# A planned attention and two gated MLPs on one core: the planner's prices and passes, and the making of the masks

## The chip, the cores and the metric

One core of a Trainium2 chip. Its engines run instruction streams of their own: TensorE (PE in the profile, its weight loads PEld), VectorE (DVE), ScalarE (ACT), GpSimd (POOL) and SyncE (SP), which issues most transfers. The metric is device microseconds of one execution of the whole program.

## The reference

Windowed attention over 2 batches, 8 heads and 768 rows: each row sees the 96 rows up to itself and the first 8 keys, with a bias that falls with the distance at a slope of its own for each head. Then two gated MLPs.

```python
def _attn_ref(q, k, v, n_global, n_local):
    scores = scale * np.matmul(q, k.transpose(0, 1, 3, 2))
    rel = pos[:, None] - pos[None, :]
    is_global = pos[None, :] < int(n_global)
    is_local = (rel >= 0) & (rel < int(n_local))
    keep = is_global | is_local
    dist = np.where(is_global & ~is_local, float(n_local), np.abs(rel).astype(np.float32))
    slopes = 2.0 ** (-8.0 * (np.arange(H, dtype=np.float32) + 1) / H)
    scores = np.where(keep, scores - slopes[:, None, None] * dist, -1000000000.0)
    scores = scores - np.max(scores, axis=-1, keepdims=True)
    a = np.exp(scores)
    a = a / (np.sum(a, axis=-1, keepdims=True) + 1e-09)
    return np.matmul(a, v)

x = attention, heads side by side                            # 2 x 768 x 512
gate = sigmoid(causal convolution of x, 5 taps, conv_w)
x = (gate * (x @ w_val)) @ w_out                             # 512 -> 512
h = relu(x @ w_in)                                           # 512 -> 1024
gate = sigmoid(centred convolution of h, 3 taps, conv_w)
out = (h * gate) @ w_out2                                    # 1024 -> 512
```

## The kernel before

The attention is done in twelve tiles of 128 rows (six a batch). A tile has its scores against its own and the previous 128 keys (`scores`, s on the page; the first 8 keys are copied into the keys that a tile reads, `first_keys`, L474). VectorE adds the head's mask and takes the row's extreme in one instruction (`least`, L441), ScalarE makes the exponentials with their sum (`grow`), GpSimd adds the small constant (`guard`, L457), VectorE inverts the sum (`invert`, L460) and scales each head (`on_dve`, L467). TensorE transposes the heads (`turn`, L491, tile t), ScalarE copies them (L495), and TensorE multiplies by the values (`output`, L509, tile x). Scores, transposes and output use TensorE's array in different shapes: 64x128, 128x128 and 128x64 rows by columns (64\*128, 128\*128 and 128\*64 in a row of the page). The first tile of a batch has only its own 128 keys (masks b, or `B0`), the others 256 (masks `B`). The former are made from a distance `d0`, the latter from `d`, by one instruction of GpSimd a head (`mask_head`).

The MLPs go over four chunks (two a batch, 400 and 368 columns with their overlap). `hidden_inputs` splits x into two parts of lower precision and starts the gate; `values` multiplies by w_val; `hidden` multiplies by W, the product of the first w_out and w_in that `product` makes on the chip; `project` multiplies by the last w_out. A large product is three matmuls (`mm3`, L219 to L221), of a high part and a remainder (`split_ops`: ScalarE L210, VectorE L212; tiles gx, gg and g). A gate (`conv_gate`) has its first tap on ScalarE (L616) or on GpSimd (L617), its further taps on VectorE (L621) and a tanh on ScalarE; VectorE multiplies by it. Weights come as 64-bit floats and are rebuilt as 32-bit ones by four instructions (`to_f32`: ScalarE, GpSimd L240, VectorE L245 and L248).

What runs when is not the program's order. Every piece is a `Work` with an engine and a price (or several engines with a price each), and a `Plan` lays them out before anything is issued. A pass from the end backward (`lay(..., True)`) gives each its rank; a pass forward takes, on the engine that is free first, the work of the least rank among those that can start, at its price, with a delay of `LAG` between engines and 0.1 for a change of TensorE's array (`SWITCH`). `issue` then emits all work in the order of the planned starts, and each engine keeps to that order. The prices are simple formulas:

```python
def act_us(n, psum=False, sums=False):
    return 0.115 + 0.000714 * n + 0.09 * sums

def pool_us(n):
    return 0.12 + 0.0018 * n
```

A load has a price of 0.5 on SyncE and a delay of 2 to 4 until it has landed. The buffers are rings (`c.ring`): four banks of PSUM for s, one each for t and x, two for f; two buffers `o` for what leaves at the end. The last block of 128 output rows goes in two halves of 256 columns, the second copied by VectorE (L771) into an `o` that must have been written out before.

## Time and profile before

| | |
|---|---|
| median of 3 runs | 297.78 us (297.34 to 299.58) |
| the profiled execution | 296.97 us |
| its span in the profile | 295.2 us |
| TensorE busy | 271.7 us, 92% of the span |
| VectorE busy | 238.3 us, 81% |
| ScalarE busy | 198.8 us, 67% |
| GpSimd busy | 57.4 us, 19% |

The span is what the trace shows from its first to its last record; the execution's time has 1.8 us around it. A busy share is one over the whole span, and where in it an engine has no gap is read from stretches of 10 us.

### The profile page before, as it was taken

To read this page: it belongs to the slowest core of one execution; us is meant where nothing else is said; L and a number is where in the kernel's file an instruction comes from. 1 tells how busy PE (TensorE), PEld (TensorE's weight loads), DVE (VectorE), ACT (ScalarE), POOL (GpSimd) and SP (SyncE) were. 2 spreads that over 40 slices of the span, in tenths; PEclk is the share of its full clock that TensorE was granted. 3 is DMA by queue.
4 is the path that set the end of the run, shared out by engine and by line. 5 is a ranking of instruction groups with operands and counts; after the bars stand their busy time and mean duration, and the time that the engine had idled before them with its cause. 6 is when DMAs were issued, how large, how long until landed. Compare 5 with 4: busy or idle time off the path is not lost.

```text
span 295.2 us, 5444 instructions
## 1 busy us (share of the span) xinstructions
PE 271.7 (92%) x1832; PEld 227.5 (77%) x1832; DVE 238.3 (81%) x638; ACT 198.8 (67%) x498; POOL 57.4 (19%) x153
## 2 busy tenths in 40 slices
PE   2398897999998999999999999999999999999990
PEld 2366775664554699999898899989999988999890
DVE  4789998899999999999799999999996643367500
ACT  2589999998386879798689663895466523466410
POOL 2831112234211210032212440011220200000000
PEclk9999999999999999999999999999999999999998
DMA  4953478564514521002412000000000000000111
GB/s 139 361 221 112 149 255 273 180 194 163 165 52 142 154 107 38 19 2 95 151 49 71 2 1 36 3 0 36 36 2 37 36 2 36 36 2 3 71 73 44
DMA packets 10277, 26.18 MB, mean 89 GB/s; under 512 B 1408, under 2 KB 2688, under 8 KB 10240
## 3 DMA queue, kind: packets, MB, share of 16 engines
q1 hardware_dynamic: 9440, 25.22, 25.1%
q10 hardware_dynamic: 800, 0.52, 0.6%
q8 instruction: 16, 0.26, 0.4%
q14 instruction: 21, 0.17, 0.2%
HBM read 22.59 MB, written 3.15 MB: 87 GB/s over the span
## 4 chain that ended last, share of the span: by engine, by line
PE 75%; DMA 8%; ACT 5%; issue 4%; DVE 3%; SPq 2%; POOL 1%; POOLq 0%; DVEq 0%; ACTq 0%
PE f L295 8%; PE f L219 8%; PE s L220 7%; PE s L221 7%; PE s L219 7%; PE f L221 7%; PE f L220 7%; PE x L509 4%; PE t L491 3%; PE s L430 3%; ACT p L446 3%; DMA v<-in_v_dram 3%; PE x L221 2%; PE t L221 2%; PE x L219 2%
## 5 line engine op out<-in xcount | busy, mean ns | idle before, releaser
L446 ACT ACTIVATE p<-p,st 128x256 f32<-128x256 f32 (+1 forms) x96 | 46.0, 483 | 7.8 <-DVE st L441 7.7
L621 DVE SCALAR_TENSOR_TENSOR z<-h,cw,z 128x384 f32<-128x384 f32 x64 | 39.9, 633 | 8.5 <-ACT z L616 7.1
L220 PE MATMUL s<-w,g 128*128 128x512 f32 (+1 forms) x104 | 39.5, 379 | 0.0
L221 PE MATMUL s<-w,g 128*128 128x512 f32 (+1 forms) x104 | 39.2, 377 | 0.0
L219 PE MATMUL s<-w,g 128*128 128x512 f32 (+1 forms) x104 | 39.1, 376 | 0.0
L623 ACT ACTIVATE z<-z 128x384 f32<-128x384 f32 (+2 forms) x48 | 25.0, 523 | 18.8 <-DVE z L621 18.8
L491 PE MATMUL t<-ident,p 128*128 128x128 f32 x176 | 29.0, 284 | 8.9 <-DVE p L467 4.8
L621 DVE SCALAR_TENSOR_TENSOR z<-x,cw,z 128x400 f32<-128x400 f32 (+1 forms) x64 | 36.9, 616 | 0.0
L491 PEld LDWEIGHTS t<-ident,p 128*128 128x128 f32 x176 | 20.2, 142 | 20.5 <-ACT pts L495 8.5
L441 DVE CUSTOM_DVE_ANT_0 p<-s,B 128x256 f32<-128x256 f32 x80 | 30.9, 414 | 3.7 <-POOL kq L474 1.4
L467 DVE TENSOR_SCALAR p<-p,st 128x256 f32<-128x256 f32 (+1 forms) x96 | 31.8, 369 | 0.4
L295 PE MATMUL f<-w,w 128*128 128x512 f32 x64 | 30.8, 604 | 0.0
L495 ACT ACTIVATE pts<-t 128x512 f32<-128x512 f32 (+1 forms) x48 | 26.5, 551 | 5.6 <-PE t L491 3.6
L219 PE MATMUL f<-gg,Wh 128*128 128x400 f32 (+1 forms) x80 | 27.7, 347 | 0.0
L221 PE MATMUL f<-gg,Wl 128*128 128x400 f32 (+1 forms) x80 | 27.1, 338 | 0.0
L220 PE MATMUL f<-gg,Wh 128*128 128x400 f32 (+1 forms) x80 | 27.0, 338 | 0.0
L212 DVE TENSOR_TENSOR g<-z,g 128x384 fp32r<-128x384 f32 x32 | 17.4, 551 | 9.9 <-ACT g L210 9.9
L430 PE MATMUL s<-kq 64*128 64x128 f32 x320 | 24.1, 289 | 0.5 <-POOL kq L474 0.5
L430 PEld LDWEIGHTS s<-kq 64*128 64x128 f32 x320 | 20.3, 193 | 4.7 <-issue 2.7
L509 PE MATMUL x<-pts,v 128*64 128x128 f32 x320 | 22.1, 278 | 2.0 <-ACT x L526 1.2
L240 POOL TENSOR_SCALAR raw<-raw 128x512 f32<-128x512 f32 x24 | 18.1, 757 | 28.9 <-ACT m L238 19.3
L734 DVE SCALAR_TENSOR_TENSOR z<-z,h 128x384 f32<-128x384 f32 x32 | 18.0, 565 | 5.7 <-ACT z L623 5.6
(117 smaller groups left out, 595.2 us busy)
## 6 DMA issues: line engine op xcount, KB each, us to landing
raw<-in_moe_w_out_dram SPq DMA_DIRECT2D x12, 512.0 KB, 3.5
kq<-in_kq_dram SPq DMA_DIRECT2D x11, 512.0 KB, 4.7
raw<-in_moe_w_in_dram SPq DMA_DIRECT2D x8, 512.0 KB, 4.0
v<-in_v_dram SPq DMA_DIRECT2D x11, 256.0 KB, 4.5
...
raw<-in_moe_w_val_dram SPq DMA_DIRECT2D x4, 512.0 KB, 3.4
...
```

Source lines behind the costliest of these rows:

```text
L219: nc.tensor.matmul(out, lh, rh, start=first, stop=False)
L220: nc.tensor.matmul(out, lh, rl, start=False, stop=False)
L221: nc.tensor.matmul(out, ll, rh, start=False, stop=last)
L295: nc.tensor.matmul(ps.t, big["wot"].t.bitcast(F32)[:, e, cs], big[wi].t.bitcast(F32)[:, e, :], start=e == 0, stop=e == 3)
L430: nc.tensor.matmul(out, keys(t0, pr, 1)[hs], keys(j, pr, 0)[hs], start=True, stop=True)
L441: nc.vector.tensor_tensor_reduce(w.t[:, :nk], sc, bias, -QKSCALE, 3.0e38, ALU.add, ALU.min, st.t[:, 0, h : h + 1])
L446: nc.scalar.activation(w.t[:, :nk], w.t[:, :nk], AF.Exp, bias=st.t[:, 0, h : h + 1], scale=-1.0, accum_out=st.t[:, 1, h : h + 1],)
L467: nc.vector.tensor_scalar(w.t[:, :nk], w.t[:, :nk], st.t[:, 2, h : h + 1], None, ALU.mult)
L491: nc.tensor.transpose(o[:, z, n, :], p[2 * pr + z].t[:, n * P : (n + 1) * P], ident)
L495: nc.scalar.activation(w.t[:, :, :nw, :], o[:, :, :nw, :], AF.Copy)
L509: nc.tensor.matmul(o[z * D : (z + 1) * D, pr, :], vals(j, 2 * pr + z), pts[pr].t[:, z, n, :], start=n == 0, stop=n == len(js) - 1,)
L621: nc.vector.scalar_tensor_tensor(z(), src(k), w()[:, k : k + 1], z(), ALU.mult, ALU.add)
```

## The change

The planner: new prices for each kind of instruction (ScalarE dearer for a sum, for a scale and for a source in SBUF; a tap on GpSimd 0.17 + 0.0013 a column instead of 0.12 + 0.0018), loads priced by their kilobytes with one delay of 2.4 until they have landed, and times at which the engines can begin (`START`). `lay` adds 3.0 to the rank of TensorE's work that would change the array's shape (`STICK`). `issue` repeats the two passes six times, each backward pass with the ends of the forward pass before as its ranks, and keeps the order, and the choice of engines, of the pass whose planned end is earliest.

The masks: GpSimd writes the positions as floats at once, with those behind the row replaced by a large number (`positions`); VectorE makes the first distance in three instructions instead of eight and the second (`distance`) in three instead of five. Each head's mask may be made by GpSimd, ScalarE or VectorE, as the planner chooses (`head_ways`, `any`); the first two heads are no longer made ahead of the branch that picks this arm of the kernel.

```diff
@@ -84,7 +85,10 @@
 
 
     LAG = {"PE": 0.2, "ACT": 0.15, "DVE": 0.15, "POOL": 0.15, "SP": 0.0}
+    START = {"DVE": 0.4, "ACT": 1.2, "SP": 0.3}
     SWITCH = 0.1
+    STICK = 3.0
+    PASSES = 6
 
     def __init__(self):
         self.work, self.wrote, self.read, self.rings = [], {}, {}, []
...
+    def any(self, ways, bufs=(), reads=(), writes=()):
+        e = next(iter(ways))
+        us, fn = ways.pop(e)
+        return self.add(e, us, fn, bufs, reads, writes, **ways)
+
...
@@ -131,6 +140,7 @@
         left = {w: len(pred(w)) for w in self.work}
         ready = {e: [] for e in self.LAG}
         free = dict.fromkeys(self.LAG, 0.0)
+        free.update({} if back else self.START)
         mode, est, at = None, dict.fromkeys(self.work, 0.0), {}
 
         def enter(w):
...
@@ -150,7 +160,7 @@
                 ws = [w for w in ws if len(w.ways) == 1 or here(w, e)]
                 if ws:
                     t = max(free[e], min(est[w] for w in ws)) + 0.02
-                    w = min((w for w in ws if est[w] <= t), key=rank)
+                    w = min((w for w in ws if est[w] <= t), key=lambda w: rank(w) + (self.STICK if not back and e == "PE" and w.mode != mode else 0.0))
                     t = max(free[e], est[w])
                     if best is None or t < best[0]:
                         best = t, w, e
...
@@ -177,23 +187,33 @@
         self.link()
         order = list(self.work)
         if laid:
-            back = self.lay(lambda w: w.succ, lambda w: w.pred, lambda w: 0.0, True)
-            for w in self.work:
-                w.rank = -back[w] - w.cost + w.bias
-            at = self.lay(lambda w: w.pred, lambda w: w.succ, lambda w: w.rank, False)
-            order.sort(key=lambda w: at[w])
+            after, best = dict.fromkeys(order, 0.0), None
+            for _ in range(self.PASSES):
+                back = self.lay(lambda w: w.succ, lambda w: w.pred, lambda w: -after[w], True)
+                for w in order:
+                    w.rank = -back[w] - w.cost + w.bias
+                at = self.lay(lambda w: w.pred, lambda w: w.succ, lambda w: w.rank, False)
+                after = {w: at[w] + w.cost for w in order}
+                end = max(after.values())
+                if best is None or end < best[0]:
+                    best = end, at, {w: w.eng for w in order}
+            end, self.at, engs = best
+            for w in order:
+                w.eng = engs[w]
+                w.cost = w.ways[w.eng][0]
+            order.sort(key=lambda w: self.at[w])
         for w in order:
             for b in w.opens:
                 b.t = b.ring.make()
             w.ways[w.eng][1]()
 
 
-def act_us(n, psum=False, sums=False):
-    return 0.115 + 0.000714 * n + 0.09 * sums
-
-
-def dve_us(n, extra=0.07):
-    return extra + 0.00104 * n
+def act_us(n, sbuf=True, scaled=False, sums=False):
+    return 0.05 + 0.000834 * n + 0.042 * sbuf + 0.092 * scaled + 0.093 * sums
+
+
+def dve_us(n, scaled=False):
+    return 0.069 + 0.001042 * n + 0.061 * scaled
 
 
 def pe_us(n):
...
@@ -201,15 +221,19 @@
 
 
 def pool_us(n):
-    return 0.12 + 0.0018 * n
-
-
-def split_ops(c, hi, lo, src, n, bufs, reads, writes):
+    return 0.17 + 0.0013 * n
+
+
+def dma_us(kb):
+    return max(0.4, kb / 385.0)
+
+
+def split_ops(c, hi, lo, src, n, bufs, reads, writes, sbuf=True):
 
...
-    pl.add("ACT", act_us(n), lambda: nc.scalar.activation(hi(), src(), AF.Copy), bufs, reads, [writes + ("hi",)])
+    pl.add("ACT", act_us(n, sbuf), lambda: nc.scalar.activation(hi(), src(), AF.Copy), bufs, reads, [writes + ("hi",)])
...
@@ -326,13 +350,18 @@
 def scratch(c):
 
     x = [c.x[:, d, XP:] for d in range(NC1)]
-    c.rel, c.ge, c.loc, c.d = (x[d][:, 0:WIN] for d in range(4))
-    c.key, c.k0, c.d0, ic = (x[d][:, 4 * P : 5 * P] for d in range(4))
-    return c.d.bitcast(I32), ic.bitcast(I32)
-
-
-def mask_head(c, out, d, h):
-    c.nc.gpsimd.tensor_scalar(out, d, -slope(h) / QKSCALE, 1.0, ALU.mult, ALU.mult)
+    c.rel, c.w, c.d = (x[d][:, 0:WIN] for d in range(3))
+    c.key, c.far, c.d0 = (x[d][:, 4 * P : 5 * P] for d in range(3))
+
+
+def positions(c):
+
+    nc = c.nc
+    nc.gpsimd.iota(c.rel, pattern=[[-1, WIN]], base=P, channel_multiplier=1, allow_small_or_imprecise_dtypes=True)
+    nc.gpsimd.iota(c.key, pattern=[[1, P]], base=0, channel_multiplier=0, allow_small_or_imprecise_dtypes=True)
+    nc.gpsimd.affine_select(
+        out=c.rel, in_=c.rel, compare_op=ALU.is_ge, fill=BIG, base=P, pattern=[[-1, WIN]], channel_multiplier=1
+    )
 
 
 def first_mask(c):
@@ -341,38 +370,40 @@
     lf = c.small.tile([P, 2], F32, name="lf")
     nc.vector.tensor_copy(lf, c.li[:, :, 0])
     c.ng, c.nl = ng, nl = lf[:, 0:1], lf[:, 1:2]
-    rel, loc, key, k0, d0 = c.rel, c.loc, c.key, c.k0, c.d0
-    nc.vector.scalar_tensor_tensor(loc, rel, nl, c.ge, ALU.is_lt, ALU.mult)
-    nc.vector.scalar_tensor_tensor(d0, rel[:, P:], nl, loc[:, P:], ALU.subtract, ALU.mult)
-    nc.vector.scalar_tensor_tensor(k0, key, ng, loc[:, P:], ALU.is_lt, ALU.max)
-    nc.vector.tensor_scalar(k0, k0, -BIG, BIG, ALU.mult, ALU.add)
-    nc.vector.scalar_tensor_tensor(d0, d0, nl, k0, ALU.add, ALU.add)
-    c.b0 = c.const.tile([P, 2, P], F32, name="b0")
-    c.B0 = [c.b0[:, h, :] for h in range(2)]
-    for h in range(2):
-        mask_head(c, c.B0[h], d0, h)
+    rel, w = c.rel[:, P:], c.w[:, P:]
+    nc.vector.tensor_scalar(c.far, c.key, ng, BIG, ALU.is_ge, ALU.mult)
+    nc.vector.scalar_tensor_tensor(w, rel, nl, c.far, ALU.is_ge, ALU.mult)
+    nc.vector.scalar_tensor_tensor(c.d0, rel, nl, w, ALU.min, ALU.add)
+
+
+def head_ways(c, n, out, d, h):
+
+    nc, k = c.nc, -slope(h) / QKSCALE
+    return {
+        "POOL": (0.02 + pool_us(n), lambda: nc.gpsimd.tensor_scalar(out(), d, k, 1.0, ALU.mult, ALU.mult)),
+        "ACT": (act_us(n), lambda: nc.scalar.activation(out(), d, AF.Copy, scale=k)),
+        "DVE": (0.07 + 0.00052 * n, lambda: nc.vector.tensor_scalar(out(), d, k, None, ALU.mult)),
+    }
 
 
 def masks(c, ap):
 
     nc, pl = c.nc, c.plan
-    ng, nl, rel, loc, d, key = c.ng, c.nl, c.rel, c.loc, c.d, c.key
+    ng, nl, rel, w, d = c.ng, c.nl, c.rel, c.w, c.d
     c.B = ap.tile([P, NH, WIN], F32, name="B")
-    b0 = ap.tile([P, NH - 2, P], F32, name="b02")
-    c.B0 += [b0[:, h, :] for h in range(NH - 2)]
-    for h in range(2, NH):
-        pl.add("POOL", 0.33, lambda h=h: mask_head(c, c.B0[h], c.d0, h), [], ["d0"], [("B0", h)])
+    b0 = ap.tile([P, NH, P], F32, name="b0")
+    c.B0 = [b0[:, h, :] for h in range(NH)]
+    for h in range(NH):
+        pl.any(head_ways(c, P, lambda h=h: c.B0[h], c.d0, h), [], ["d0"], [("B0", h)])
 
     def distance():
-        nc.vector.tensor_scalar(key[:, 0:GW], key[:, 0:GW], ng, None, ALU.is_lt)
-        nc.vector.tensor_scalar(d, loc, -BIG, BIG, ALU.mult, ALU.add)
-        nc.vector.tensor_scalar(d[:, 0:GW], key[:, 0:GW], -BIG, BIG, ALU.mult, ALU.add)
-        nc.vector.tensor_tensor(d[:, GW:], d[:, GW:], rel[:, GW:], ALU.add)
-        nc.vector.tensor_scalar(d[:, 0:GW], d[:, 0:GW], nl, None, ALU.add)
-
-    pl.add("DVE", 1.1, distance, [], [], ["d"])
+        nc.vector.tensor_scalar(w[:, GW:], rel[:, GW:], nl, BIG, ALU.is_ge, ALU.mult)
+        nc.vector.scalar_tensor_tensor(d[:, GW:], rel[:, GW:], nl, w[:, GW:], ALU.min, ALU.add)
+        nc.vector.tensor_scalar(d[:, 0:GW], c.far[:, 0:GW], nl, None, ALU.add)
+
+    pl.add("DVE", 0.75, distance, [], [], ["d"])
     for h in range(NH):
-        pl.add("POOL", 0.6, lambda h=h: mask_head(c, c.B[:, h, :], d, h), [], ["d"], [("B", h)])
+        pl.any(head_ways(c, WIN, lambda h=h: c.B[:, h, :], d, h), [], ["d"], [("B", h)])
 
 
 def fast_attention(c, ap):
...
-        pl.add("SP", 0.5, lambda: nc.sync.dma_start(kq[t].t, c.kq[b, i]), [kq[t]], [], [("kq", t)], delay=4.0)
+        pl.add("SP", dma_us(512), lambda: nc.sync.dma_start(kq[t].t, c.kq[b, i]), [kq[t]], [], [("kq", t)], delay=LANDING)
...
-        "ACT", act_us(n), lambda: nc.scalar.activation(z(), src(0), AF.Copy, scale=w()[:, 0:1]), bufs, reads, [token],
+        "ACT", act_us(n, True, True), lambda: nc.scalar.activation(z(), src(0), AF.Copy, scale=w()[:, 0:1]), bufs, reads, [token],
         POOL=(pool_us(n), lambda: nc.gpsimd.tensor_scalar(z(), src(0), w()[:, 0:1], 1.0, ALU.mult, ALU.mult)),
     )
     for k in range(1, taps):
         def tap(k=k):
             nc.vector.scalar_tensor_tensor(z(), src(k), w()[:, k : k + 1], z(), ALU.mult, ALU.add)
-        pl.add("DVE", dve_us(n, 0.13), tap, bufs, reads, [token])
+        pl.add("DVE", dve_us(n, True), tap, bufs, reads, [token])
...
@@ -804,15 +835,11 @@
         nc.scalar.dma_start(k0[:, 0:2], kq[0, 0, :, 0:2])
         nc.sync.dma_start(k0[:, 2:4], kq[0, 0, :, 2:4])
         nc.scalar.dma_start(v0, v[0, 0:P].rearrange("s (a h) d -> s a h d", a=4))
-        it, ic = scratch(c)
-        nc.gpsimd.iota(it, pattern=[[-1, WIN]], base=P, channel_multiplier=1)
-        nc.gpsimd.iota(ic, pattern=[[1, P]], base=0, channel_multiplier=0)
+        scratch(c)
+        positions(c)
         nc.vector.memset(one, 0.0)
         _, (glo, ghi, llo, lhi) = nc.values_load_multi_w_load_instructions(c.nn)
         nc.scalar.activation(one, one, AF.Exp)
-        nc.vector.tensor_copy(c.rel, it)
-        nc.vector.tensor_scalar(c.ge, c.rel, 0.0, None, ALU.is_ge)
-        nc.vector.tensor_copy(c.key, ic)
         nc.gpsimd.memset(c.x[:, :, 0:XP], 0.0)
         make_identity(nc, c.ident)
         first_mask(c)
```

The prices of the other instructions that the plan knows (`to_f32`, `least`, `grow`, `copy`, `gate` and so on) change in the same way; the instructions themselves stay what they were. Of the 48 first taps GpSimd has 20 in the new plan (12 of them for the second MLP), where it had 5 (1 for the second); ScalarE has the others. TensorE's matmuls are the same ones, with 62 changes of array shape instead of 79; behind the last of 512 columns there were 27 of 256, and now 33.

VectorE ahead of its first `least` (the row L441), before. x is where the positions lie, lf the two sizes, b the first tile's masks, p and st a head's scores and its row's extreme:

```order
L347 SCALAR_TENSOR_TENSOR x<-x,lf 128x128
L348 TENSOR_SCALAR x<-x 128x128
L349 SCALAR_TENSOR_TENSOR x<-x,lf 128x128
L911 ISA
L911 REGISTER_ALU x3
L911 COMPARE_AND_BRANCH
L367 TENSOR_SCALAR x<-x,lf 128x32
L368 TENSOR_SCALAR x<-x 128x256
L369 TENSOR_SCALAR x<-x 128x32
L370 TENSOR_TENSOR x<-x 128x224
L371 TENSOR_SCALAR x<-x,lf 128x32
L441 ISA p,st<-s,b_112 128x128
```

And with the change:

```order
L371 CAST lf<-li 128x2
L374 TENSOR_SCALAR x<-x,lf 128x128
L375 SCALAR_TENSOR_TENSOR x<-x,lf 128x128
L376 SCALAR_TENSOR_TENSOR x<-x,lf 128x128
L938 ISA
L938 REGISTER_ALU x3
L938 COMPARE_AND_BRANCH
L385 TENSOR_SCALAR b_224<-x 128x128 x3
L472 ISA p,st<-s,b_224 128x128
```

The two casts and the comparison of positions are gone (L813 to L815, ahead of these rows), and of the first distance three instructions are left (L374 to L376); three heads of the first mask (L385) are VectorE's now, and the three instructions on the second distance (L400 to L402) have gone behind seven of the first tile's eight `least` (L472).

TensorE from its first matmul, before. s are scores (of x, where the first tile's keys lie, and of kq), t transposes of p, x the output:

```order
L430 MATMUL s<-x 128x128 x8
L491 MATMUL t<-ident,p 128x128 x2
L430 MATMUL s<-x,kq 128x128 x2
L430 MATMUL s<-kq 128x128 x2
L430 MATMUL s<-x,kq 128x128 x2
L430 MATMUL s<-kq 128x128 x2
L491 MATMUL t<-ident,p 128x128 x2
```

And with the change:

```order
L461 MATMUL s<-x 128x128 x8
L461 MATMUL s<-x,kq 128x128 x2
L461 MATMUL s<-kq 128x128 x2
L461 MATMUL s<-x,kq 128x128 x2
L461 MATMUL s<-kq 128x128 x2
L461 MATMUL s<-x,kq 128x128 x2
L461 MATMUL s<-kq 128x128 x2
L461 MATMUL s<-x,kq 128x128 x2
L461 MATMUL s<-kq 128x128 x2
L522 MATMUL t<-ident,p 128x128 x4
```

The sixteen matmuls of the second tile's scores (the rows with kq, half of them for four of its heads) stand ahead of the first transposes now, where a pair of transposes was ahead of each half.

GpSimd about the second and third chunk, before. raw is a weight's rebuilding, z<-x a first tap of the first MLP's gate, z<-h one of the second's, h and hb the edges of a chunk:

```order
L240 TENSOR_SCALAR raw<-raw 128x512
L709 MEMSET h 128x1
L720 COPY hb<-h 128x17
L240 TENSOR_SCALAR raw<-raw 128x512 x2
L617 TENSOR_SCALAR z<-x,cw 128x400
L711 COPY h<-hb 128x17
L712 MEMSET h 128x1
L240 TENSOR_SCALAR raw<-raw 128x512 x2
```

And with the change:

```order
L264 TENSOR_SCALAR raw<-raw 128x512
L648 TENSOR_SCALAR z<-x,cw 128x400
L648 TENSOR_SCALAR z_2092<-h,cw 128x384
L264 TENSOR_SCALAR raw<-raw 128x512
L648 TENSOR_SCALAR z_2103<-h,cw 128x384
L648 TENSOR_SCALAR z<-x,cw 128x400
L648 TENSOR_SCALAR z_2154<-h,cw 128x384
L742 COPY h<-hb 128x17
L743 MEMSET h 128x1
L742 COPY h<-hb 128x17
L743 MEMSET h 128x1
L648 TENSOR_SCALAR z_2249<-h,cw 128x384
```

Between the same weight instructions (raw) one first tap stood, and now there are six (the next weight instruction follows these rows); of the second MLP's gates (z<-h) GpSimd had one in all before, ahead of these rows.

## Rows read from the trace of the kernel before

**Rows 1.** The page, busy time, share of the span and instructions of each engine.

```profile
PE 271.7 (92%) x1832; PEld 227.5 (77%) x1832; DVE 238.3 (81%) x638; ACT 198.8 (67%) x498; POOL 57.4 (19%) x153
```

**Rows 2.** Windows: PE (twice), PEld, DVE, ACT, POOL busy; clock; DMA share; GB/s.

```profile
150.00:160.00 10.00, 10.00 (x55) 9.33 (x55) 9.74 (x19) 9.11 (x20) 2.13 (x4) 1.00 0.07 18
```

**Rows 3.** Timeline at the end: start, duration, engine, line; [idle before, releaser].

```profile
285.06 0.60 ACT L769 ACTIVATE o<-s 128x512 f32<-128x512 f32 x1 [0.50 <-PE s L221]
...
287.76 0.28 PE L221 MATMUL s<-w,g 128*128 128x256 f32 x1
...
289.92 0.42 DVE L771 TENSOR_SCALAR o<-s 128x256 f32<-128x256 f32 x1 [9.63 <-DMA out_dram<-o]
```

**Rows 4.** Timeline of TensorE's first transposes, and of VectorE from 11 to 21.

```profile
11.89 0.66 PE L491 MATMUL t<-ident,p 128*128 128x128 f32 x2 [4.84 <-DVE p L467]
...
11.07 1.07 DVE L467 TENSOR_SCALAR p<-p,st 128x128 f32<-128x128 f32 x4
...
14.60 0.42 DVE L441 CUSTOM_DVE_ANT_0 p<-s,B 128x256 f32<-128x256 f32 x1 [1.03 <-PE s L430]
...
17.45 0.42 DVE L441 CUSTOM_DVE_ANT_0 p<-s,B 128x256 f32<-128x256 f32 x1 [1.39 <-POOL kq L474]
...
18.84 0.69 DVE L245 SCALAR_TENSOR_TENSOR raw<-raw 128x512 int32<-128x512 int32 x1
19.44 0.17 DVE L460 RECIPROCAL st<-st 128x4 f32<-128x4 f32 x1
...
20.52 0.61 DVE L467 TENSOR_SCALAR p<-p,st 128x256 f32<-128x256 f32 x2
```

**Rows 5.** Timeline of VectorE and TensorE about 157 us.

```profile
156.66 0.99 DVE L212 TENSOR_TENSOR gg<-z,gg 128x368 fp32r<-128x368 f32 x2 [0.23 <-ACT gg L210]
...
157.61 0.40 PE L221 MATMUL s<-w,g 128*128 128x512 f32 x1
...
157.85 0.33 PE L219 MATMUL f<-gg,Wh 128*128 128x368 f32 x1
...
158.01 0.33 PE L220 MATMUL f<-gg,Wh 128*128 128x368 f32 x1
```

**Rows 6.** Timeline of VectorE at the start.

```profile
6.38 0.35 DVE L349 SCALAR_TENSOR_TENSOR x<-x,lf 128x128 f32<-128x128 f32 x1
7.11 0.24 DVE L367 TENSOR_SCALAR x<-x,lf 128x32 f32<-128x32 f32 x1 [0.38 <-issue]
...
8.27 0.28 DVE L441 CUSTOM_DVE_ANT_0 p<-s,b 128x128 f32<-128x128 f32 x1
...
9.96 0.08 DVE L441 DVE_READ_ACCUMULATOR2_ANT st<- 128x1 f32 x1
```

**Rows 7.** Timeline of SyncE's queue at the start.

```profile
0.74 0.38 SPq L803 DMA_DIRECT2D li<-in_n_dram  x1
...
5.41 0.34 SPq L403 DMA_DIRECT2D kq<-in_kq_dram  x1
```

**Rows 8.** DMA issues: count, KB each, median us from issue to landing.

```profile
kq<-in_kq_dram SPq DMA_DIRECT2D x11, 512.0 KB, 4.7
...
li<-in_n_dram SPq DMA_DIRECT2D x1, 2.0 KB, 3.4
```

**Rows 9.** Timeline of VectorE, two reciprocals that wait.

```profile
51.67 0.18 DVE L460 RECIPROCAL st<-st 128x4 f32<-128x4 f32 x1 [0.94 <-POOL st L457]
...
56.60 0.18 DVE L460 RECIPROCAL st<-st 128x4 f32<-128x4 f32 x1 [1.11 <-POOL st L457]
```

**Rows 10.** Timeline of GpSimd and VectorE at 158 us.

```profile
157.83 0.90 POOL L617 TENSOR_SCALAR z<-x,cw 128x400 f32<-128x400 f32 x1 [6.45 <-DVE gg L212]
...
158.18 0.96 DVE L621 SCALAR_TENSOR_TENSOR z<-h,cw,z 128x384 f32<-128x384 f32 x1
```

**Rows 11.** Lines by form: count; busy us, mean ns of one; idle before, releaser.

```profile
L621 DVE SCALAR_TENSOR_TENSOR z<-h,cw,z 128x384 f32<-128x384 f32 x64 | 39.9, 633 | 8.5 <-ACT z L616 7.1
...
L616 ACT ACTIVATE z<-h,cw 128x384 f32<-128x384 f32 x31 | 18.9, 612 | 2.3 <-DVE g L212 1.0 <-POOL h L709 0.9
```

More of the change, by code (lines that the diff above doesn't have):

```diff
@@ L237, in to_f32 @@
     tail = (token, "tail")
-    pl.add("ACT", act_us(n), lambda: nc.scalar.activation(dst(), whole(), AF.Copy, scale=2.0**-112), bufs, reads, [token])
+    pl.add("ACT", act_us(n) + 0.05, lambda: nc.scalar.activation(dst(), whole(), AF.Copy, scale=2.0**-112), bufs, reads, [token])
     pl.add(
@@ L248, in join @@
         nc.vector.scalar_tensor_tensor(bits(), bits(), 3, high(), ALU.logical_shift_left, ALU.bitwise_or)
-    pl.add("DVE", dve_us(n, 0.12), last_bits, bufs, [], [tail])
-    pl.add("DVE", dve_us(n, 0.12), join, bufs, [tail], [token])
+    pl.add("DVE", dve_us(n), last_bits, bufs, [], [tail])
+    pl.add("DVE", dve_us(n), join, bufs, [tail], [token])
 def conv_weights(c):
@@ L257, in conv_weights @@
     w = c.small.tile([P, n], F32, name="cw")
-    c.plan.add("SP", 0.5, lambda: nc.sync.dma_start(raw.rearrange("p d t -> p (d t)"), c.conv_w), writes=["cwr"], delay=2.5)
+    c.plan.add("SP", dma_us(44), lambda: nc.sync.dma_start(raw.rearrange("p d t -> p (d t)"), c.conv_w), writes=["cwr"], delay=LANDING)
     to_f32(c, lambda: w, lambda: raw, n, [], ["cwr"], "cw")
@@ L300, in product @@
                 c, lambda cb=cb, fs=fs: c.Wh[:, cb, fs], lambda cb=cb, fs=fs: c.Wl[:, cb, fs], lambda ps=ps: ps.t,
-                512, [ps], [("wps", half, cb)], ("W", half, cb),
+                512, [ps], [("wps", half, cb)], ("W", half, cb), False,
             )
@@ L498, in fast_attention @@
             pl.add("PE", 0.218 * len(js), turn, [pt] + two, [("p", t, 2 * pr), ("p", t, 2 * pr + 1)], [("pt", t, pr)])
-            pl.add("ACT", act_us(2 * nk), copy, [pt, pts[pr]], [("pt", t, pr)], [("pts", t, pr)])
+            pl.add("ACT", act_us(2 * nk, False), copy, [pt, pts[pr]], [("pt", t, pr)], [("pts", t, pr)])
             if pr % XPAIRS < XPAIRS - 1:
@@ L674, in gate @@
             nc.vector.scalar_tensor_tensor(zz.t[:, :n], zz.t[:, :n], 1.0, pv.t[:, :n], ALU.add, ALU.mult)
-        pl.add("DVE", dve_us(n, 0.13), gate, [zz, pv], [("pv", b, ch, cb)], [("z", b, ch, cb)])
+        pl.add("DVE", dve_us(n), gate, [zz, pv], [("pv", b, ch, cb)], [("z", b, ch, cb)])
         split_ops(
@@ L734, in gate @@
         nc.vector.scalar_tensor_tensor(z.t, z.t, 1.0, h.t[:, 1 : 1 + CH], ALU.add, ALU.mult)
-    pl.add("DVE", dve_us(CH, 0.13), gate, [z, h], tk, [zt])
+    pl.add("DVE", dve_us(CH), gate, [z, h], tk, [zt])
     split_ops(c, lambda: g.t[:, 0], lambda: g.t[:, 1], lambda: z.t, CH, [g, z], [zt], ("g2", b, ch, f))
@@ L771, in copy @@
                 nc.vector.tensor_scalar(o.t[:, :w], po[n].t[:, :w], 0.5, None, ALU.mult)
[L773 removed]
+        pl.add("ACT" if n < nt else "DVE", act_us(w, False), copy, [po[n], o], [("po", b, ch, n)], [("o", b, ch, n)])
         t1 = ch * CH + t * P
         pl.add(
[L776 to L777 removed]
+            "SP", dma_us(w // 2), lambda o=o, t1=t1, c0=c0, w=w: nc.sync.dma_start(c.out[b, t1 : t1 + P, c0 : c0 + w], o.t[:, :w]),
+            [o], [("o", b, ch, n)], [], delay=LANDING,
         )
```

22 lines of the change are left out of this document (10 added, 12 removed).

## The prediction

> **What bounds the kernel now.** The first view is the page: TensorE is busy for 271.7 of 295.2 us, VectorE for 238.3 [rows 1]. So TensorE idles for 23.5 us, and no order of the work can give back more than that. The stretches of 10 us say where: at 150 to 160 us TensorE has 10.00 and VectorE 9.74 [rows 2], one of seventeen stretches from 110 to 280 us in which TensorE has 10.00. Its idle time is thus ahead of 110 us and behind its last matmul (287.76 + 0.28 = 288.04 [rows 3]): 295.2 - 288.0 = 7.2 us of tail, 4.84 us before its first transposes [rows 4], 5 us before its first matmul, and some 6.5 us in small pieces.
>
> One must not stop there: a matmul at 200 us can be earlier only if what it reads is. The timeline about 157 us shows that VectorE sets it. There it writes the last two remainders `gg` of the second chunk's gated values until 156.66 + 0.99 = 157.65, and TensorE begins the matmuls of `hidden` that read them at 157.85 [rows 5]. The two engines meet there with 0.2 us between them. From that point TensorE runs without a gap to 288.04, that is 130.2 us. I call it the meeting point, and the sum is made there: when does VectorE reach it in the new order, how much TensorE work is behind it, how long is the tail.
>
> **The change part by part.**
>
> *Masks and start.* Before, VectorE ends the first distance at 6.38 + 0.35 = 6.73, the last of nine instructions; after the branch (7.11) five more for the second distance stand ahead of the first `least`, at 8.27 [rows 6]. Now the positions come from GpSimd as floats. The sizes `li` land at 0.74 + 3.4 = 4.1 [rows 7, 8]; a cast and three instructions are left. At the 0.35 of L349 for the largest, with a cast of about 0.2 and some 0.27 for the simpler one, they end at 4.1 + 0.2 + 0.27 + 0.35 + 0.35 = 5.3. The branch takes 0.38 (6.73 to 7.11), three heads of the mask, now on VectorE, about 0.25 each (as L467 on 128 columns, 1.07 for four [rows 4]): the first `least` starts at 6.5. GpSimd's part is hidden: its positions are made at the very start, while every engine still loads the sizes; a new select over 256 columns delays GpSimd's first head by some half a us at most, and three of the first four heads are VectorE's. If that cover is gone, it costs that half us.
>
> From 6.5 on I add up VectorE's new order to the place where the second tile's first four heads are scaled. Eight `least` of 128 columns took 8.27 to 10.04, 0.22 each; four L467 1.07; four `least` of 256 columns 17.45 to 18.84, or 0.35 each; a weight instruction 0.60 (18.84 to 19.44); two L467 of 256 columns 0.61; a reciprocal 0.2 [rows 4, 6]. The new row of work: 8 x 0.22 = 1.8, a fourth head 0.25, the three instructions of `distance` 0.9, a reciprocal 0.2, four L467 1.07, two heads of B 0.6, reciprocal 0.2, four L467 1.07, eight `least` 2.8, two weight instructions 1.2, reciprocal 0.2, four L467 1.2. That is 11.5, so it ends at 18.0; before, at 20.52 + 0.61 = 21.13 [rows 4]. What goes is waiting: 1.03 for scores that stood behind the first transposes (these had waited 4.84 themselves), and 1.39 for GpSimd, which made masks in one long row [rows 4]. The scores of the second tile now stand ahead of all transposes. Their keys are requested at 5.41, and the median to landing is 4.7 us [rows 7, 8], so they land at 10.1; VectorE wants the scores at 11.9. **Gain 3.1 us.** The bounds: 0.4 if the scores come as late as before (14.60, 2.7 later than wanted), 3.4 if two of the three heads are hidden behind GpSimd's first.
>
> *Work ahead of the meeting point.* Counted in the two orders from that place to the fourth `gg`, the new order has one weight instruction of each of three kinds more (3 x 0.60) and one `least` (0.35), and one conv tap and one gate less (0.53 + 0.47): **+1.2 us**. It has an answer without a range, as the order is known.
>
> *Waits of VectorE.* At 51.67 and 56.60 it waits 0.94 and 1.11 for GpSimd's guard, which waits for ScalarE's exponentials [rows 9]. In the new order more of VectorE's other work stands ahead of each such reciprocal (by 3.6 to 4.4 us of dense work at these two, where before ScalarE was 0.8 to 1.9 behind). I take both as gone: **gain 2.05**, bounds 0 and the 4.8 of all its six waits of over 0.2 us between 27 and 147 us, of which these are two.
>
> *First conv taps on GpSimd.* ScalarE gives up fifteen of them; GpSimd has 20 instead of 5, six more than before ahead of the meeting point. They are off the path as such, but not free. A tap of GpSimd's ran 157.83 to 158.73; VectorE's L621 beside it took 0.96 where its mean is 0.633 [rows 10, 11]: 0.33 lost. I take that for each of the six: **loss 2.0**, bounds 0 (where no two meet) and 5.4 (six times the 0.90 of a tap). The Trainium skill ("SBUF — State Buffer", "Who interferes with whom") has a rule that speaks against this part: a VectorE instruction with two SBUF inputs and a GpSimd instruction that reads SBUF contend for one port pair, and the later one blocks until the other is done. By that rule each tap can block VectorE for up to its own length. By bounds from rows that is the upper end; the stretched row agrees with the rule, at a third of the tap's length.
>
> *TensorE behind the meeting point.* The new order has three 512-column matmuls more there and nine 368-column ones less. Their spacing is 0.24 and 0.16 us (starts at 157.61, 157.85 and 158.01 [rows 5]): +0.7 - 1.5 = **gain 0.8**. The changes of array shape fall from 79 to 62 over the whole attention part, all ahead of that point; since VectorE sets the point, I take them at nothing. Their cover is TensorE's waits there; without VectorE as the bound they would be worth some more.
>
> *Tail.* The last copy waits on VectorE until 289.92 for the second last full output to leave its buffer; that copy began at 285.06, 27 matmuls of 256 columns ahead of TensorE's end at 288.04 [rows 3], 0.114 us each. The new order has 33 behind the same output: 6 x 0.114 = **gain 0.7**, as the buffer comes free that much earlier before TensorE's end. What is late next is TensorE's own last matmul, still 1.2 us ahead of that copy.
>
> *Sum.* -3.1 + 1.2 - 2.05 + 2.0 - 0.8 - 0.7 = -3.45. VectorE reaches the meeting point at 157.65 - 1.95 = 155.7; TensorE ends 130.2 - 0.8 = 129.4 us behind it, 0.2 apart as before, at 285.3; with a tail of 6.5 the span is 291.8. The profiled execution took 296.97, that is 1.8 more than its span, and the median of the runs is 297.78, so I take the difference from the median: 297.78 - 3.45 = 294.3 us.
>
> **The rivals.**
>
> *Faster.* VectorE waits nowhere between 27 and 147 us (4.8 gone instead of 2.05), and the taps don't meet it: -3.1 + 1.2 - 4.8 - 0.8 - 0.7 = -8.2, or 289.6 us. For it speaks that ScalarE loses fifteen taps of 0.61 us [rows 11]; against it, that two engines this full have always some wait.
>
> *Given back.* The start is gained, but the waits of 2.05 turn up elsewhere, and the taps cost their 2.0: -3.1 + 1.2 + 2.0 - 0.8 - 0.7 = -1.4, or 296.4. The same time comes if the planner's prices don't hold (0.69 us for a tap that took 0.90, a load of 512 KB that lands after 3.7 where the median is 4.7) and its order is no better than the old one but for the start. For it speaks how full VectorE is [rows 2].
>
> *Slower.* GpSimd becomes the bound behind the meeting point. All fifteen extra taps lie in the stretch in which VectorE is full; each blocks it for 0.33, and each comes 0.29 later than from ScalarE (0.90 for 0.61), with VectorE's next tap queued behind it and TensorE waiting for the gate: 15 x 0.62 = 9.3. With -3.1 + 1.2 - 0.8 - 0.7 = -3.4 that is +5.9, or 303.7. It decides from 0.23 us a tap on (3.4 / 15), at which the kernel is not faster any more. For it speaks the stretched row [rows 10]; against it, that nine of the taps stand behind the meeting point, where VectorE's results are ready earlier before they are read.
>
> **How the numbers follow.** The forecast has 0.40, given back 0.31, faster 0.15, slower 0.14. The forecast's own range is 292.0 to 296.5. The range is 289.5 to 299.5: it takes in the faster case, the one given back, and the slower one up to half of its price. A measurement of this kernel tells about 1% (3 us) from no change; the forecast at 1.2% lies near that bound. Faster by over 1% (below 294.8): 0.15 and three quarters of 0.40, 0.45 in all. Slower by over 1% (above 300.8): 0.10 of the 0.14. Within: 0.45.
>
> **What would show it.** VectorE's first `least` at 6.5 us and the scaling of the second tile's first heads done by 18; no wait of about 1 us for GpSimd's guard between 40 and 60; 20 taps on GpSimd, with VectorE instructions of 0.9 to 1.0 us beside them; the fourth `gg` of the second chunk by 155.7; TensorE's end at 285.3 and 6.5 us behind it. The prediction is wrong if TensorE shows gaps of over 1 us behind 150 us (GpSimd or VectorE late for it), or if it meets VectorE well before the point, so that its fewer changes of shape pay.

## The result and the profile after

The changed kernel takes **288.96 us** (median of 4 runs, 288.44 to 288.99) where the kernel before took 297.7 beside it: a ratio of 0.969, 95% interval 0.965 to 0.973. The forecast was 294.3 us, its range ended at 289.5, and the gain is 8.7 us instead of 3.45. Medians here and below are of all runs of a kernel; ratios and their intervals leave out the few runs in a slower state, at a lower granted clock (two of ten in e5).

The page's busy times after, to be held against [rows 1]:

```profile
PE 269.2 (94%) x1832; PEld 228.0 (79%) x1832; DVE 238.6 (83%) x637; ACT 192.6 (67%) x486; POOL 68.5 (24%) x160
```

VectorE is busy for as long as before, ScalarE for 6 us less and GpSimd for 11 us more: taps have gone from one to the other. TensorE's 1832 matmuls are the same and the span is 8.0 us shorter (287.2). Counted on TensorE, whose first matmul is at 4.97 in both traces, 2.2 of the 8.0 went from the tail, 3.3 from its idle time between its first and last matmul (11.4, now 8.1) and 2.5 from the time for which the same matmuls are busy. The windows show where, after (first two lines) and before (last two): us, TensorE (twice), its loads, VectorE, ScalarE, GpSimd, clock, DMA share, GB/s.

```profile
0.00:100.00 100.00, 86.94 (x719) 60.33 (x720) 93.24 (x334) 81.18 (x244) 28.36 (x66) 1.00 0.59 194
100.00:287.00 187.00, 182.22 (x1115) 167.70 (x1113) 145.37 (x304) 111.39 (x243) 40.12 (x94) 1.00 0.11 36
...
0.00:100.00 100.00, 84.10 (x698) 55.81 (x700) 88.54 (x316) 77.43 (x232) 27.41 (x69) 1.00 0.54 181
100.00:295.00 195.00, 187.56 (x1140) 171.71 (x1136) 149.79 (x323) 121.32 (x268) 30.02 (x84) 0.99 0.12 41
```

In the first 100 us VectorE does 4.7 us more work than before, and TensorE 2.8 more by busy time (21 matmuls more). From 100 us on TensorE idles for 4.8 instead of 7.4 us, nearly all of it the tail.

The start on VectorE's timeline, for [rows 6] and the end of [rows 4] (start, duration, engine, line, operation):

```profile
5.22 0.35 DVE L376 SCALAR_TENSOR_TENSOR x<-x,lf 128x128 f32<-128x128 f32 x1
6.03 0.72 DVE L385 TENSOR_SCALAR b<-x 128x128 f32<-128x128 f32 x3 [0.45 <-DVE x L376]
6.66 0.28 DVE L472 CUSTOM_DVE_ANT_0 p<-s,b 128x128 f32<-128x128 f32 x1
...
17.20 1.14 DVE L498 TENSOR_SCALAR p<-p,st 128x256 f32<-128x256 f32 x4
```

The first `least` is at 6.66 (6.5 was forecast), and the second tile's first heads are scaled at 17.20 + 1.14 = 18.34 (18.0), against 21.13 before. TensorE's start:

```profile
9.08 0.80 PE L461 MATMUL s<-x,kq 64*128 64x128 f32 x4 [2.03 <-DVE x L401]
...
12.80 0.44 PE L522 MATMUL t<-ident,p 128*128 128x128 f32 x2
```

The scores of the second tile begin at 9.08, ahead of all transposes, as its keys land (the row names an instruction of VectorE, but the keys, asked for at 5.41, landed 3.5 us later, at 8.95). Then the meeting point, for [rows 5]:

```profile
151.73 0.33 PE L243 MATMUL f<-gg,Wh 128*128 128x368 f32 x1
...
151.96 0.53 DVE L236 TENSOR_TENSOR gg<-z,gg 128x368 fp32r<-128x368 f32 x1
```

VectorE ends the fourth `gg` at 152.49 (157.65 before, 155.7 forecast). TensorE's first matmul of that `hidden` starts 0.76 us ahead of it, since its first nine matmuls read earlier `gg`. The chain of work that ended last (start, length, piece) passes from VectorE to TensorE 72 us ahead of that; behind the last row here it is TensorE's down to the last copy, but for one copy of ScalarE's (0.61 at 90.00):

```profile
80.09 0.61 DVE Wl L236
80.70 0.04 issue
80.75 3.27 PE f L319 x7
```

Before, it passed to TensorE earlier still, and was TensorE's down to the tail, but for one copy of ScalarE's and one of GpSimd's:

```profile
61.59 0.28 ACT pts L495
61.91 0.44 PE t L491 x2
...
91.38 0.60 ACT x L526
...
100.50 0.31 POOL kq L474
...
285.68 4.02 DMA out_dram<-o
```

In neither trace does VectorE stand in the chain at the meeting point.

The tail, for [rows 3]:

```profile
278.56 0.60 ACT L800 ACTIVATE o<-s 128x512 f32<-128x512 f32 x1 [0.45 <-PE s L245]
...
281.94 0.28 PE L245 MATMUL s<-w,g 128*128 128x256 f32 x1
...
282.31 0.42 DVE L802 TENSOR_SCALAR o<-s 128x256 f32<-128x256 f32 x1 [8.82 <-PE s L245]
```

TensorE ends at 282.22. The last copy follows it at once and no longer waits for an output buffer; 5.0 us stand behind TensorE's end, where 7.2 stood.

Who waited for whom (engine, line, what it waited for: us in all, times, longest), VectorE between the scaled heads and the meeting point, after (waits of over 0.15 us):

```profile
DVE raw L269 <- POOL h L740: 1.1, 2, 0.6
DVE w L236 <- ACT w L234: 0.3, 1, 0.3
DVE st L491 <- POOL st L488: 0.2, 1, 0.2
```

and before, the four largest:

```profile
DVE st L460 <- POOL st L457: 2.1, 2, 1.1
DVE w L212 <- ACT w L210: 1.1, 1, 1.1
DVE z L734 <- ACT z L623: 0.8, 1, 0.8
DVE p L441 <- PE t L491: 0.8, 2, 0.6
```

### The profile page after: what moved, and what is told of

Same layout as the page of the kernel before. It is cut to its first block, busy times and chain, and to the rows that moved or that the text cites. A ratio compares the mean times of both kernels' runs of the same rounds, so it can differ in the third digit from the quotient of the medians.

```text
span 287.2 us, 5402 instructions
## 1 busy us (share of the span) xinstructions
PE 269.2 (94%) x1832; PEld 228.0 (79%) x1832; DVE 238.6 (83%) x637; ACT 192.6 (67%) x486; POOL 68.5 (24%) x160
## 4 chain that ended last, share of the span: by engine, by line
PE 72%; DVE 20%; issue 3%; DMA 2%; ACT 1%; POOL 1%; SPq 0%; DVEq 0%; POOLq 0%
PE s L244 8%; PE s L245 8%; PE s L243 8%; PE f L243 7%; PE f L245 7%; PE f L244 7%; DVE p L472 5%; DVE p L498 4%; PE s L461 4%; PE x L540 4%; PE t L522 4%; DVE raw L269 3%; PE t L243 2%; PE x L245 2%; PE t L245 2%
## 5 line engine op out<-in xcount | busy, mean ns | idle before, releaser
L652 DVE SCALAR_TENSOR_TENSOR z<-h,cw,z 128x384 f32<-128x384 f32 x64 | 40.6, 643 | 12.6 <-ACT z L647 10.9
L652 DVE SCALAR_TENSOR_TENSOR z<-x,cw,z 128x400 f32<-128x400 f32 (+1 forms) x64 | 38.4, 628 | 0.1
L498 DVE TENSOR_SCALAR p<-p,st 128x256 f32<-128x256 f32 (+1 forms) x96 | 31.1, 368 | 0.7
L472 DVE CUSTOM_DVE_ANT_0 p<-s,B 128x256 f32<-128x256 f32 x80 | 30.7, 417 | 0.4 <-PE t L522 0.4
L319 PE MATMUL f<-w,w 128*128 128x512 f32 x64 | 30.1, 601 | 0.7 <-DVE Wl L236 0.6
L461 PE MATMUL s<-kq 64*128 64x128 f32 x320 | 25.0, 291 | 0.5 <-DVE st L472 0.5
L461 PEld LDWEIGHTS s<-kq 64*128 64x128 f32 x320 | 21.0, 194 | 5.5 <-issue 3.2
L648 POOL TENSOR_SCALAR z<-h,cw 128x384 f32<-128x384 f32 x12 | 11.4, 947 | 49.1 <-DVE z L652 31.0
L245 PEld LDWEIGHTS s<-w,g 128*128 128x128 f32 x104 | 19.5, 188 | 3.8
```

What stands on the lines that cost most here:

```text
L245: nc.tensor.matmul(out, ll, rh, start=False, stop=last)
L319: nc.tensor.matmul(ps.t, big["wot"].t.bitcast(F32)[:, e, cs], big[wi].t.bitcast(F32)[:, e, :], start=e == 0, stop=e == 3)
L461: nc.tensor.matmul(out, keys(t0, pr, 1)[hs], keys(j, pr, 0)[hs], start=True, stop=True)
L472: nc.vector.tensor_tensor_reduce(w.t[:, :nk], sc, bias, -QKSCALE, 3.0e38, ALU.add, ALU.min, st.t[:, 0, h : h + 1])
L498: nc.vector.tensor_scalar(w.t[:, :nk], w.t[:, :nk], st.t[:, 2, h : h + 1], None, ALU.mult)
L652: nc.vector.scalar_tensor_tensor(z(), src(k), w()[:, k : k + 1], z(), ALU.mult, ALU.add)
```

## The experiments

Times are medians; the ratio is to the kernel before on the same chip (296.8 to 297.8 us), with its 95% interval. "Another order" is the price of a change of shape at 0.12 instead of 0.10. "Loads" are the prices of all transfers on SyncE, the writes of the outputs among them. Kernels on different chips are compared by their ratios where it comes to 1 us.

| kernel | us | ratio | in another order |
|---|---|---|---|
| before | 297.7 | 1 | 296.41, 0.995 (0.991 to 0.998) |
| masks alone | 301.00 | 1.013 (1.008 to 1.017) | 295.32, 0.991 (0.985 to 0.996) |
| loads alone | 295.51 | 0.994 (0.992 to 0.997) | |
| masks and loads | 290.04 | 0.977 (0.975 to 0.979) | 293.18, 0.984 (0.978 to 0.989) |
| the change | 288.96 | 0.969 (0.965 to 0.973) | 290.81, 0.979 (0.977 to 0.982) |
| without the masks | 292.62 | 0.985 (0.982 to 0.989) | |
| without the loads' prices | 295.49 | 0.994 (0.991 to 0.997) | 294.59, 0.992 (0.991 to 0.994) |
| without the engines' prices | 289.21 | 0.974 (0.972 to 0.976) | |
| without the shape penalty | 293.53 | 0.988 (0.986 to 0.990) | 291.84, 0.979 (0.973 to 0.984) |
| with one pass | 292.40 | 0.984 (0.980 to 0.988) | |
| taps on ScalarE | 289.68 | 0.975 (0.971 to 0.978) | |

**e1, masks alone.** The kernel before with the functions `scratch` to `masks` of the change, GpSimd's heads at their old price:

```diff
-    pl.add("POOL", 0.33, lambda h=h: mask_head(c, c.B0[h], c.d0, h), [], ["d0"], [("B0", h)])
+    pl.any(head_ways(c, P, lambda h=h: c.B0[h], c.d0, h), [], ["d0"], [("B0", h)])
```

> The kernel before with the new masks (positions, three instructions for each distance, each head's mask by any of three engines) and its old planner with its old prices. If the start is worth what the prediction's first term says (3.1 us) whatever the planner does, 294 to 295 us, with the first least at about 6.6 us and the second tile's first heads scaled about 3 us earlier than 21.13. If the new prices and passes are what carries an early start on to the end, the early start is lost to VectorE's and TensorE's later waits and the time is 296 to 298. If the masks are the whole gain, 289 to 290.

Slower, 301.0 us. Its chief waits on TensorE, in the view of waits (of an execution that took 304.1, the longest of five):

```profile
PE x L521 <- DMA v<-in_v_dram: 7.0, 3, 3.1
PE s L442 <- DMA x<-in_kq_dram: 5.0, 1, 5.0
PE t L503 <- DVE p L479: 3.9, 1, 3.9
```

The wait of about 5.0, for the first keys, stands in every kernel; the 7.0 for loads of the values was 0.8 before. On the timeline of SyncE and TensorE:

```profile
29.42 0.38 SPq L533 DMA_DIRECT2D v<-in_v_dram  x1
...
35.21 1.97 PE L521 MATMUL x<-pts,v 128*64 128x128 f32 x16 [2.40 <-DMA v<-in_v_dram]
37.11 1.12 PE L503 MATMUL t<-ident,p 128*128 128x128 f32 x4
...
43.99 1.09 PE L521 MATMUL x<-pts,v 128*64 128x128 f32 x16
```

The load, of 64 KB, went out at 29.42, just behind one of 512 KB, and landed at 35.2, 5.7 us later, where the planner had reckoned with 2.5. And the wait costs more than its 2.4 us: the sixteen matmuls behind it took 1.97, and the same sixteen at 43.99 took 1.09. The granted clock shows it: 0.72 of 2.4 GHz in the mean of 30 to 40 us, so part of that stretch ran at 1.2 GHz. TensorE had stood still for 2.4 us before.

**e2, the planner alone.** The changed kernel with the old functions `scratch` to `masks`:

```diff
-        scratch(c)
-        positions(c)
+        it, ic = scratch(c)
```

> The changed kernel with the old masks: their nine and five instructions on VectorE, every head's mask by GpSimd, planner as changed. If the masks carry 3 us of the gain of 8.7, about 292. If the planner alone carries all of it, 289 to 290. If the planner is worth nothing without the early start, as the prediction's sum has it (its other terms add to -0.35), 297.

292.62: the masks are worth 3.7 us to the new planner (4.9 by the ratios), against the 3.1 of the forecast's first term, and the planner 4.5 without them. The forecast's sum without its first term leaves the planner 0.35, so it was far too small there.

**e3, one pass.**

```diff
-    PASSES = 6
+    PASSES = 1
```

> The changed kernel with one backward and one forward pass instead of six. If the repeated passes are what closes the waits, 292 to 296. If the prices (and the delay of a load) close them, within 1 us of 289.

292.40, 3.4 slower than the change. With 2 to 12 passes the order comes out as with six: the second pass is the one kept. As two orders of one planner lie up to 5.7 us apart (below), this run alone doesn't show that the second pass is the cause.

**e4, taps on ScalarE.** The change's order, with the taps moved from GpSimd to ScalarE at their places.

```diff
-                w.eng = engs[w]
+                w.eng = "ACT" if set(w.ways) == {"ACT", "POOL"} else engs[w]
```

> The changed kernel's order with all twenty of GpSimd's first taps done by ScalarE at the same places of the order. If each tap costs VectorE 0.33 us, as the prediction's fourth term has it, and VectorE sets the meeting point, 287 (six taps ahead of it, 2 us). If the taps on GpSimd are off the path, as the trace after has it (TensorE dense from 80.75 us on), within 1 us of 289. If they relieve ScalarE where it is late, slower: 290 to 293.

289.68, within 1 us: where the twenty taps run is worth less than 1 us. VectorE reaches the meeting point at 153.47, 1.0 later than with the taps on GpSimd.

**e5 and e18, loads priced as before**, in two orders. One of six such lines, the last of them the outputs':

```diff
-    c.plan.add("SP", dma_us(512), dma, [raw], [], [("raw", raw)], delay=LANDING)
+    c.plan.add("SP", 0.5, dma, [raw], [], [("raw", raw)], delay=4.0)
```

> The changed kernel with the loads priced as before (0.5 us on SyncE whatever their size, delays of 2 to 4). The masks alone made the kernel slower, with TensorE waiting 7.0 us for loads of the values. If pricing loads by their bytes is what lets the planner use the early start, waits for loads come back and the time is 292 to 297. If the other prices and the passes do it, within 1 us of 289.

295.49. TensorE waits for loads of the values again (second row):

```profile
PE s L461 <- DMA x<-in_kq_dram: 5.0, 1, 5.0
PE x L540 <- DMA v<-in_v_dram: 3.5, 3, 2.1
PE t L522 <- DVE p L498: 3.2, 1, 3.2
```

This execution took 293.4; the ten runs spread from 292.67 to 297.16, eight of them up to 295.82, those of the change by 0.6.

> The changed kernel with the loads priced as before, in another order (0.12 instead of 0.10). If old prices of loads cost several us in any order, by TensorE's waits for loads of the values, 293 to 297 again. If the 295.5 was scatter, 289 to 292.

294.59, slower again, but by another way: TensorE waits only 0.8 for the values, VectorE reaches the meeting point at 156.59, and the tail is 6.9 us where the change in that order (e17) has 4.9. So the loss is shown twice, and its mechanism differs with the order: here two of the 3.0 us between the two profiles are the tail.

**e6, old prices of the engines**, in `act_us`, `dve_us` and `pool_us`:

```diff
-    return 0.17 + 0.0013 * n
+    return 0.12 + 0.0018 * n
```

> The changed kernel with the old price formulas of ScalarE, VectorE and GpSimd; loads, passes, start times, shape rule and masks as changed (the choice of engine then gives GpSimd 6 taps instead of 20). If the engines' measured prices close VectorE's waits, 292 to 295. If loads and passes do, within 1 us of 289.

289.21: the engines' measured prices are worth nothing here.

**e7 and e15, no shape penalty**, in two orders.

```diff
-    STICK = 3.0
+    STICK = 0.0
```

> The changed kernel without the penalty for changing the array's shape. As the prediction has it (changes of shape cost nothing, because VectorE sets the meeting point), within 1 us of 289. If TensorE is what is late ahead of 90 us, some 17 more changes at about 0.1 us each: 290.5 to 291.5.

> The changed kernel without the shape penalty, in another order (0.12 instead of 0.10). If the penalty itself is worth 4 us, 292.5 to 294.5 again. If the 293.5 was scatter, 289 to 291.5.

293.53 and 291.84, with 84 and 78 changes of shape where the change has 62 and 63. Against the change in the same two orders (288.96 and 290.81) that is 4.6 and 1.0 us. The first is slower; in the second the ratios to the kernel before are alike (0.979 and 0.979), so a loss is not shown there, and the penalty's worth is not settled.

**e8, e9, e13 and e14: masks and loads on the old planner.** e9 has the loads' prices alone, e8 both; e13 is e1 and e14 is e8 in another order.

```diff
-    c.plan.add("SP", 0.5, dma, [raw], [], [("raw", raw)], delay=4.0)
+    c.plan.add("SP", dma_us(512), dma, [raw], [], [("raw", raw)], delay=LANDING)
```

> The kernel before with the new masks and with loads priced by their bytes; the other prices, the two single passes and the rest of the old planner kept. If the prices of loads are what the masks alone lacked, TensorE's waits for loads go and the time is 292 to 295. If they are not, it stays at 299 to 302.

> The kernel before with loads priced by their bytes and nothing else changed. With the new masks this price took the time from 301.0 to 290.0. If it is worth that much by itself, whatever the masks, 289 to 291; if it is worth what the changed kernel loses without it, 291 to 293; if it only mends what the earlier start spoils, within 1.5 us of 297.

> The kernel before with the new masks alone, in another order (price of a change of shape 0.12 instead of 0.10). If it is the old price of loads that spoils the early start, TensorE waits for loads of the values again and the time is 298 to 302. If the 301.0 was an unlucky order, 293 to 297.

> The kernel before with the new masks and loads priced by their bytes, in another order (0.12 instead of 0.10). If these two parts carry the gain, 289 to 291.5 again. If the 290.0 was a lucky order, 292 to 296.

290.04, 295.51, 295.32 and 293.18. The two parts together give 6.8 and 4.6 us with two single passes, no penalty and old engine prices; each by itself gives 1.3 (loads) or between a loss of 3.9 and a gain of 2.5 (masks). The gain of e9 is all in the tail (5.7 us for 7.2): TensorE ends at 288.18 there, and at 288.04 before. That masks alone do harm fell with e13: 301.0 was one bad order.

**e10, a third output buffer** for the kernel before, in its own order.

```diff
-            c.ring["o"] = sb(late_pool, "o", [P, DM], F32, 2)
+            c.ring["o"] = pl.ring(2, lambda: late_pool().tile([P, DM], F32, tag="o", name="o", bufs=3))
```

> The kernel before in the very same order, with a third buffer for what leaves at the end, so that the last copy need not wait for the second last full output to be written (289.92 where TensorE ended at 288.04). If that wait is the whole of the tail's loss, the tail falls from 7.2 to about 5.3 us and the time by 1.9. If TensorE or the last transfer sets it anyway, no difference.

294.69, 2.1 less, as expected; the tail is 4.8 us.

**e11, e12 and e17: other orders** of the kernel before (0.12), of the change (penalty 4.0) and of the change (0.12):

```diff
-    SWITCH = 0.1
+    SWITCH = 0.12
```

> The kernel before with one number of its planner moved by little, the price of a change of shape from 0.10 to 0.12, which gives another order without any better knowledge of the chip. If the price of an order is known to the planner, within 1 us of 297. If orders of like planned length differ by several us on the chip, and some of what separates the kernels is that scatter, 294 to 301.

> The changed kernel with the penalty for a change of shape at 4.0 instead of 3.0, another order of like planned length. If the changed planner's orders are alike on the chip, within 1 us of 289; if they scatter as far as the removal of the penalty moved them (293.5), 287 to 294.

> The changed kernel in another order (price of a change of shape 0.12 instead of 0.10). If the full change holds its gain whatever the order, 288.5 to 290.5. If 289.0 is one lucky order, 291 to 294.

296.41, 289.77 and 290.81. The change keeps a gain of 6.2 us or more in each of three orders. The 288.96 is the best of them, by 0.8 and 1.9 us.

**e16, two banks for transposes**, one for f:

```diff
-BANKS = {"s": 4, "t": 1, "x": 1, "f": 2}
+BANKS = {"s": 4, "t": 2, "x": 1, "f": 1}
```

> The changed kernel with two PSUM banks for transposes and one for f instead of one and two. If TensorE's 4.7 us of waits for ScalarE's copies come from the one bank and count, 285 to 287. If they move to other waits (the f bank is needed by the products and by the first MLP), 288 to 292.

289.98: the waits for ScalarE's copies (4.7 us in the change) went, and waits for VectorE's scaled heads came in their place (6.1 us). No kernel tried here beats the change.

## Why the prediction was wrong

**The step that failed in the mechanism is "VectorE sets it".** The matmul at 157.85 starts 0.24 us behind the one at 157.61 [rows 5], which is their spacing: the 0.2 us between the two engines were no wait. In the chain of before TensorE leads from 61.91 on. Its last two stops were for ScalarE and GpSimd (start, duration, engine, line, then idle time before it and what ended it):

```profile
92.03 1.09 PE L509 MATMUL x<-pts,v 128*64 128x128 f32 x16 [1.18 <-ACT x L526]
...
94.02 0.60 PE L491 MATMUL t<-ident,p 128*128 128x128 f32 x4
94.45 1.88 PE L295 MATMUL f<-w,w 128*128 128x512 f32 x4
96.17 0.60 PE L491 MATMUL t<-ident,p 128*128 128x128 f32 x4
96.70 1.10 PE L509 MATMUL x<-pts,v 128*64 128x128 f32 x16
...
100.85 1.16 PE L430 MATMUL s<-kq 64*128 64x128 f32 x16 [0.47 <-POOL kq L474]
```

Behind 100.85 it has no gap, so on this trace an earlier `gg` in the same order of TensorE's work would have brought nothing; no run tried it. What can bring something is an order in which TensorE stops less and changes shape less. The rows give the price of a change: four transposes take 0.43 us to the next start ahead of a matmul of the same shape (94.02 to 94.45), and 0.53 ahead of one of another (96.17 to 96.70). At that 0.10 the 17 fewer changes make 1.7 us, an estimate, and TensorE's busy time fell by 2.5. The prediction took them at nothing "since VectorE sets the point", and named this among its signs of being wrong: TensorE meets VectorE well before the point. The runs without the penalty (e7, e15) don't settle how much of it reaches the end.

The sum can still be held against the trace term by term, because much the same work of TensorE stands behind the point in every order: in all twenty profiles TensorE ends 128.5 to 131.0 us behind VectorE's fourth `gg` (129.7 in the change, 130.4 before). That says where the two stand, not which of them sets the time; it splits the same 8.0 us as the account on TensorE does, and the two don't add up. Three terms came out near what was said:

- the start, -3.1: it was -2.8 (18.34 for 21.13);
- the further work, +1.2: +1.1, counted from the trace by the median of each kind of instruction;
- TensorE's work behind the point, -0.8: -0.7.

**Three terms were mis-sized, and all to the same side.** From the scaled heads to the fourth `gg` VectorE's time can be split into idle time (waits of over 0.15 us), the median length of each kind of instruction, and what is over it, the stretching. Idle time went from 5.5 to 1.6, that is -3.9 where "I take both as gone: gain 2.05" was written; the upper bound of 4.8 was the better choice. The stretching went from 7.1 to 7.5, so +0.4 where the taps' **loss 2.0** stood. The row of the stretched tap was read rightly, and such rows are there after too: a tap of GpSimd's, and beside it an instruction of the weights' rebuilding that took 0.97 where the twelve of its kind have a mean of 0.775:

```profile
143.51 0.97 POOL L648 TENSOR_SCALAR z<-x,cw 128x400 f32<-128x400 f32 x1 [1.08 <-DVE gg L236]
...
144.05 0.97 DVE L272 SCALAR_TENSOR_TENSOR m<-m,raw 128x512 int32<-128x512 int32 x1
...
L272 DVE SCALAR_TENSOR_TENSOR m<-m,raw 128x512 int32<-128x512 int32 x12 | 9.3, 775 | 0.2
```

But I priced the six new meetings and not the old ones. Ahead of the point, six instructions of VectorE are stretched beside taps, by 1.3 us in all, and those beside GpSimd's part of the weights' rebuilding (14 before, 12 after) lose 1.6 to 2.0 less than before. With all taps on ScalarE (e4) the stretching is 7.3 us, the same. The rows agree with the rule of the Trainium skill ("SBUF — State Buffer", "Who interferes with whom"), but what the program loses by it is not the number of GpSimd's instructions times a price.

The **tail** gave 2.2 us where 0.7 stood. The new order does put 33 matmuls behind the second last full output instead of 27, and its buffer does come free that much earlier. But I kept the transfer's 4.0 us. The landing times of the outputs in the last stretch, before and after:

```profile
DMA to landing us min/median/max: 1.9/2.0/4.0
...
DMA to landing us min/median/max: 2.0/2.3/3.0
```

The 4.0 is that one write, asked for 2.35 us ahead of TensorE's end. In all profiles with loads priced by bytes it is asked for 2.8 to 3.0 us ahead and lands after 2.0 to 2.1; in the other seven, asked for 2.35 to 2.40 ahead, it took 3.9 to 4.3 in five and 2.2 in two. What holds it there was not tried, and the time of asking alone does not decide it. With 2.0 the wait goes altogether. The tail's 2 us come with the price of the transfers, in either planner (5.0 in e8, 5.7 in e9), or with a third buffer (e10); e5, with the old prices, has 5.0 too, since its write landed after 2.2.

Together: 0.3 less at the start, 1.9 more in waits, 1.6 in stretching and 1.5 in the tail make 4.7 more than the forecast's 3.45, or 8.1; the span is 8.0 shorter.

**The step that is missing** is SyncE's queue of transfers. The prediction has no term for the loads' prices; it names them only among reasons why the gain might be given back. They decide whether it is kept: with the old prices the change is worth 1.3 and 2.5 us (e5, e18) instead of 8.7 and 6.2, and masks with loads alone already give 4.6 to 6.8. With old prices a load is placed 2.5 to 4 us ahead of its reader, whatever stands in the queue, and in e1 that was not kept (5.7); what is won at the start is then lost at a load, a late output or a worse order. The rival "given back" had the right place for the danger and the wrong sign, since pricing by bytes removes it. The rival "faster" (289.6) comes closest: no waits and no loss by taps; it had a chance of 0.15. Its number agrees in part by luck: its waits are 0.9 too long and its tail 1.5 too short.

What stays open is the share of the penalty and of the second pass. Kernels that differ by that one number of the planner alone (0.10 and 0.12) lie 0.4 to 5.7 us apart, and one or two orders for each kernel can't separate 1 to 4 us from that. The 8.7 is itself the best of the change's three orders.
